# Sink products of two head pairs side by side at half depth, and a new order of the later steps

## The chip, the cores and the metric

The kernel runs on one core of one Trainium2 chip. The metric is the device time of one execution in microseconds (us); less is better. The times shown for a kernel are medians of several executions.

## What is computed

The reference is a windowed attention with sink columns, followed by a gated MLP block that also mixes along the sequence. Sizes: 4 batches, 8 heads, 768 positions, head size 64, so a model width of 512; the MLP is 1024 wide, in two halves of 512. Every query position sees the 4 first positions (the sinks) and the last 128 positions up to itself. All arrays come in as float32.

```python
# attention, for each batch and head
scores = q @ k.T / 8
keep = (pos_k < 4) | ((pos_q - pos_k >= 0) & (pos_q - pos_k < 128))
a = softmax(where(keep, scores, -1e9)); x = a @ v        # heads side by side: x is 768 x 512
# block, for each batch
h = gelu_tanh(x @ w_in); u, v = h[:, :512], h[:, 512:]
v_n = (v - mean(v)) / sqrt(var(v) + 1e-6) * g_ln
v_s = w_sg @ v_n + b_sg[:, None]                         # w_sg is 768 x 768, over positions
out = x + (u * v_s) @ w_out
```

## The kernel before

The work is written as a list of 669 steps, the string `STEPS`. A loop at the end (L675 to L680) runs through it and calls for each step the function of that name, so the list alone sets the order of the instructions on every engine. Each engine takes its own instructions strictly in that order; between engines semaphores make an instruction wait for data and for a buffer to come free. The batches overlap: while TensorE does the block of one batch, the attention of the next is loaded and begun.

The sequence is six tiles of 128 positions, the heads are four pairs (p = 0 to 3). The steps, with b for the batch:

- `LQ.b.i`, `LK.b.i`, `LVH.b.i`, `LWO` are loads. GpSimd (POOL) issues them with a cast to bfloat16, each taking its turn in POOL's queue. `TQ`, `TK` turn q and k with TensorE, `EQ`, `EK` copy the result out of PSUM (suffix A: ScalarE, D: VectorE). In the last batch `DQ`, `DK` turn by DMA, issued by SyncE (SP).
- `QK.b.p.g` (L473) makes the scores of pair p for two query tiles, with the two heads in the two halves of TensorE's rows (64 rows each). `EX` (L486) is the exponential on ScalarE (ACT). `MK` (L490) applies the window mask, on VectorE (DVE, suffix D, L495) or in two instructions on POOL (suffix P, L498 and L501).
- `SK.b.g` (L458) makes the scores of the 4 sink columns of all heads at once for the tiles 2 to 5; head h stands in rows 16h to 16h+3 of one tile, so pair p has rows 32p to 32p+31. `SX` (L465) is their exponential, into `exs`.
- `AV.b.p.k` (L512) multiplies the weights with v into a PSUM tile `mm`: for the batches 1 to 3, k = 0 holds the query tiles 0 to 2 and k = 1 the tiles 3 to 5. For each query tile from 2 on, one product over all 128 rows of `exs` with `v_sink` adds the sinks (L531); `v_sink` is zero outside the pair's own rows. `NR` (L536) divides by the row sums and writes `x_sb` (DVE, two instructions).
- `XD.b.half` (L555) turns `x_sb` by DMA (SP). `MV`, `MU` (L562, L603) are the two halves of x @ w_in, `GV`, `GU` their gelu on ACT; `BN`, `RS`, `NM`, `Z` are the normalization (DVE; `RS` on POOL; `Z` on DVE or ACT by suffix).
- `WT`, `WE` turn w_sg. `SP.b.hf.dc` (L624) is w_sg times the normalized half for three position tiles (hf) and 128 channels (dc); `GT` (L631, DVE) brings it out of PSUM into one of four buffers `gtmp`; `GM` (L636) multiplies with u on DVE or POOL. `OU.b.t` (L640) is the product with w_out, `RA` (L647, DVE) adds x, `ST` and `SH` store (SP). The very last tile is done in two column halves of 256: `OH.3.5.h` (L653), `RH.3.5.h` (L660), `SH.3.5.h`.
- `TBL` (L308) is a one-element activation on ACT, which brings the table of the exponential (E) or of gelu (G) into the engine.

PSUM is two rings: `sc_ring`, two tiles of two banks (`QK`, `MV`, `MU`), and `mm_ring`, four tiles of one bank (everything else). A ring hands out its tiles in the order in which the steps ask (`fresh`, L187). The product that writes into a tile waits for the reader of what that tile held four turns before (two for `sc_ring`). The rings in SBUF work alike, `gtmp` with 4 buffers and `P` (the weights after `EX`) with 10.

Of the kernel before, what the change touches and what calls it, by code (L numbers as in the profile page):

```python
# [40 lines left out]
AV.1.2.1 EX.2.1.0 GM.0.1.2.P NR.1.1.1 AV.1.3.1 NR.1.2.1 QK.2.2.0 LK.3.0 QK.2.3.0 EX.2.2.0 OU.0.1 NR.1.3.1 GM.0.1.3.P  # L41
EX.2.3.0 TBL.G OU.0.2 XD.1.1 RA.0.1 GM.0.1.1.P TK.2.2 MK.2.3.0.D TQ.2.1 LVH.2.0 TQ.2.2 EQ.2.1.D MV.1.0 EQ.2.2.D LQ.3.0
EK.2.2.D LQ.3.1 VSM.2 MU.1.0 GV.1.0 MK.2.1.0.D LVH.2.1 BN.1.0 MV.1.1 GU.1.0 LQ.3.2 RA.0.2 LQ.3.3 MK.2.0.0.D MV.1.2
GV.1.1 MK.2.2.0.D LK.3.1 KS.2 LK.3.2 BN.1.1 MU.1.1 GV.1.2 LK.3.3 BN.1.2 RS.1.1 MU.1.2 GU.1.1 LQ.3.4 NM.1.1 Z.1.0.A
RS.1.2 OU.0.3 GU.1.2 TBL.E LQ.3.5 NM.1.2 Z.1.1.D SK.2.0 Z.1.4.D QK.2.0.1 Z.1.2.D Z.1.3.A QK.2.1.1 Z.1.5.D OU.0.4
# [20 lines left out]
SP.3.0.0 GM.3.1.2.D SP.3.0.1 GT.3.0.0 GT.3.1.3 SP.3.0.2 GT.3.0.1 GM.3.1.3.P SP.3.0.3 GM.3.0.0.D GM.3.0.1.P GT.3.0.2
OU.3.3 GM.3.0.2.D GT.3.0.3 OU.3.4 GM.3.0.3.D RA.3.3 OU.3.0 RA.3.4 ST.3.3 OU.3.1 RA.3.0 ST.3.4 OU.3.2 ST.3.0 RA.3.1
OH.3.5.0 OH.3.5.1 ST.3.1 RA.3.2 ST.3.2 RH.3.5.0 SH.3.5.0 RH.3.5.1 SH.3.5.1
# [8 lines left out]
def kernel(  # L77
# [412 lines left out]
    def MK(b, p, g, e="D"):  # L490
        w = wide(g)
        pt = P[b, p, g]
        if e == "D":
# [4 lines left out]
        nc.gpsimd.affine_select(out=p4[:, :, :, 0:128], in_=p4[:, :, :, 0:128], compare_op=ALU.is_ge,  # L498
                                fill=0.0, base=0, pattern=[[0, 2], [0, 2], [1, 128]],
                                channel_multiplier=-1)  # L500
        nc.gpsimd.affine_select(out=p4[:, :, :, 128:256], in_=p4[:, :, :, 128:256],  # L501
                                compare_op=ALU.is_ge, fill=0.0, base=-1,
                                pattern=[[0, 2], [0, 2], [-1, 128]], channel_multiplier=1)
# [7 lines left out]

    def AV(b, p, k):  # L512
        vb = v_sb[b]
        fresh(mm_ring, ("a", b, p, k))
        av = av_view(b, p, k)
        i0, n = rowsof(b, k)
        first = True
        for il in range(n):
            i = i0 + il
            for hl in range(2):  # L520
# [5 lines left out]
                if i >= 1:  # L526
                    c = 128 if i % 2 else 384
                    nc.tensor.matmul(av[:, il, hl, :], pt[:, hl, c:c + 128], vb[:, h, i - 1, :],  # L528
                                     start=False, stop=(i < 2 and il == n - 1 and hl == 1))
# [186 lines left out]
```

## Time and profile before

| | us |
|---|---|
| median of 3 runs (lowest, highest) | 155.58 (155.23, 155.91) |
| the profiled execution | 155.89 |
| its span, first to last instruction | 154.2 |
| TensorE products (PE) busy | 145.7 |
| VectorE (DVE) busy | 122.9 |
| ScalarE (ACT) busy | 100.0 |
| GpSimd (POOL) busy | 99.7 |

The span starts with the first instruction and ends with the last; 1.7 us of the profiled execution lie around it. Starts are measured. The ends of matmuls are modelled, and a matmul's duration there holds its way through the array, in which the next one already runs. So the pace of a stream of matmuls is read from the starts, and "idle" on PE is less than the gap between two starts.

### The profile page before, as it was taken

The numbers are of one execution on the slowest core, as the hardware profiler recorded it, in microseconds if no ns is written. First come the engines' busy times: TensorE is split into PE (matmuls) and PEld (weight loads), VectorE is DVE, ScalarE is ACT, GpSimd is POOL, SyncE is SP. The second block draws the span as 40 slices with busy tenths as digits, with TensorE's granted clock in tenths as the row PEclk, the third lists the DMA queues.
The fourth block names the chain that finished last, engine by engine and source line by source line (L and its number), as shares of the span: only waits on it lengthen the run. The fifth ranks groups of instructions, "written<-read, shape, count | busy, mean of one in ns | idle before, by whom it ended". The sixth has DMA issues, their size and how long they took to land.

```text
span 154.2 us, 3867 instructions
## 1 busy us (share of the span) xinstructions
PE 145.7 (95%) x1540; PEld 94.5 (61%) x1554; DVE 122.9 (80%) x296; ACT 100.0 (65%) x117; POOL 99.7 (65%) x127
## 2 busy tenths in 40 slices
PE   6899899999999988999899999999999999999990
PEld 2355586879675765758466764486567644775550
DVE  4666889739989977797799887899789957867992
ACT  3699998799899766456987865369957122491000
POOL 4099799298999699999469769640798610400400
PEclk9999999999999999999999999999999999999999
DMA  4999999999999999999999399996510582410055
GB/s 158 305 351 157 154 195 204 166 189 211 148 141 154 185 155 140 147 150 156 156 223 250 81 276 177 185 190 81 211 72 1 105 221 73 150 54 20 0 203 206
DMA packets 87178, 24.67 MB, mean 160 GB/s; under 512 B 78772, under 2 KB 84920, under 8 KB 87160
## 3 DMA queue, kind: packets, MB, share of 16 engines
q0 software_dynamic: 64608, 11.01, 95.7%
q1 hardware_dynamic: 22552, 13.41, 33.0%
q8 instruction: 12, 0.20, 0.5%
q14 instruction: 6, 0.05, 0.1%
HBM read 24.81 MB, written 6.29 MB: 202 GB/s over the span
## 4 chain that ended last, share of the span: by engine, by line
PE 54%; POOL 18%; DMA 15%; ACT 4%; DVE 4%; issue 2%; SPq 1%; DVEq 0%; ACTq 0%; POOLq 0%
PE mm L627 15%; DMA v_sb<-in_v_dram 11%; PE mm L644 10%; PE sc L566 9%; PE sc L607 8%; POOL q L225 5%; POOL k L225 4%; DMA uT<-in_k_dram 4%; PE sc L483 4%; PE mm L524 3%; POOL v_sb L271 3%; PE mm L528 2%; POOL wsg_gated L637 2%; POOL P L498 2%; POOL P L501 2%
## 5 line engine op out<-in xcount | busy, mean ns | idle before, releaser
L488 ACT ACTIVATE P<-sc 128x1024 bf16<-128x1024 f32 (+1 forms) x48 | 43.4, 952 | 10.3 <-PE sc L483 10.1
L627 PE MATMUL mm<-wsgT,z 128*128 128x384 bf16 x192 | 34.4, 327 | 0.3 <-ACT z L597 0.3
L627 PEld LDWEIGHTS <-z 128*128 128x128 bf16 x192 | 17.6, 98 | 12.5 <-issue 0.7
L570 ACT ACTIVATE vt<-sc 128x1024 f32<-128x1024 f32 x12 | 12.3, 1027 | 18.4 <-PE sc L566 18.4
L632 DVE SCALAR_TENSOR_TENSOR gtmp<-mm,g_sb,b_bc 128x384 bf16<-128x384 f32 x32 | 19.0, 610 | 4.2 <-PE mm L627 4.0
L637 POOL TENSOR_TENSOR wsg_gated<-gtmp,uT 128x384 bf16<-128x384 bf16 x15 | 14.9, 1006 | 11.3 <-DVE gtmp L632 11.2
L607 PE MATMUL sc<-xT,w_in_sb 128*128 128x256 bf16 x192 | 22.1, 273 | 0.0
L566 PE MATMUL sc<-w_in_sb,xT 128*128 128x512 bf16 x92 | 21.8, 379 | 0.2
L644 PE MATMUL mm<-w_out_sb,wsg_gated 128*128 128x512 bf16 x85 | 21.2, 379 | 0.5
L498 POOL TENSOR_SCALAR_AFFINE_SELECT P<-P 128x512 bf16<-128x512 bf16 x21 | 13.7, 653 | 11.4 <-ACT P L488 11.4
L607 PEld LDWEIGHTS <-w_in_sb 128*128 128x128 bf16 x192 | 18.7, 98 | 2.9
L579 DVE BATCH_NORM_STATS2 st<-vt 128x6 f32<-128x512 f32 x24 | 15.4, 685 | 6.1 <-ACT vt L570 6.0
L541 DVE TENSOR_TENSOR x_sb<-mm,rcp 128x384 bf16<-128x384 f32 (+1 forms) x36 | 18.5, 513 | 1.2
L588 POOL TENSOR_TENSOR rs<-rs,neg_half 128x4 f32<-128x4 f32 (+1 forms) x8 | 7.1, 882 | 15.8 <-DVE rs L583 14.4
L225 POOL DMA_DIRECT2D k<-in_k_dram x18 | 16.4, 924 | 1.3 <-DMA v_sb<-in_v_dram 1.3
L648 DVE TENSOR_TENSOR ot<-mm,x_sb 128x512 f32<-128x512 f32 x23 | 15.4, 683 | 2.2 <-PE mm L644 2.2
L225 POOL DMA_DIRECT2D q<-in_q_dram x18 | 16.8, 956 | 0.0
L524 PE MATMUL mm<-v_sb,P 128*128 128x65 bf16 x192 | 16.1, 194 | 0.6 <-DVE x_sb L541 0.4
L524 PEld LDWEIGHTS <-P 128*128 128x128 bf16 x192 | 14.5, 97 | 2.5 <-DMA v_sb<-in_v_dram 0.6
L528 PE MATMUL mm<-v_sb,P 128*128 128x65 bf16 x160 | 15.4, 193 | 0.4 <-POOL P L501 0.4
L612 ACT ACTIVATE uT<-sc 128x1024 bf16<-128x1024 f32 x12 | 12.2, 1024 | 5.1 <-PE sc L607 5.1
L566 PEld LDWEIGHTS <-xT 128*128 128x128 bf16 x96 | 9.2, 98 | 10.1
(92 smaller groups left out, 242.9 us busy)
## 6 DMA issues: line engine op xcount, KB each, us to landing
out_dram<-ot SPq DMA_DIRECT2D x17, 256.0 KB, 2.5
v_sb<-in_v_dram POOLq DMA_DIRECT2D x8, 384.0 KB, 8.0
q<-in_q_dram POOLq DMA_DIRECT2D x18, 128.0 KB, 6.5
k<-in_k_dram POOLq DMA_DIRECT2D x18, 128.0 KB, 7.3
out_dram<-ot SPq DMA_DIRECT2D x14, 128.0 KB, 1.8
wsg_gated<-in_moe_w_sg_dram POOLq DMA_DIRECT2D x2, 576.0 KB, 8.4
w_in_sb<-in_moe_w_in_dram POOLq DMA_DIRECT2D x2, 512.0 KB, 9.0
uT<-in_q_dram SPq DMA_DIRECT2D x2, 384.0 KB, 3.0
```

The source lines that it names most:

```text
L225: return nc.gpsimd.dma_start(out=dst.rearrange("p (h d) -> p h d", h=H), in_=heads(src, b, i))
L488: nc.scalar.activation(out=P.new((b, p, g))[:, :, 0:w], in_=sc_ring[b, p, g][:, :, 0:w], func=AF.Exp, scale=scale)
L498: nc.gpsimd.affine_select(out=p4[:, :, :, 0:128], in_=p4[:, :, :, 0:128], compare_op=ALU.is_ge, fill=0.0, base=0, pattern=[[0, 2], [0, 2], ...
L524: nc.tensor.matmul(av[:, il, hl, :], pt[:, hl, c:c + 128], vb[:, h, i, :], start=first, stop=False)
L528: nc.tensor.matmul(av[:, il, hl, :], pt[:, hl, c:c + 128], vb[:, h, i - 1, :], start=False, stop=(i < 2 and il == n - 1 and hl == 1))
L541: nc.vector.tensor_mul(x_sb.get(b)[:, i0:i0 + n, 128 * p:128 * (p + 1)].rearrange("p t (h d) -> p t h d", h=2), av[:, :, :, 0:Dh], rcp[:, ...
L566: nc.tensor.matmul(hp[:, jl, :], xT[b][:, 2 * g + jl, c, :], w_in_sb[:, c, d_half:2 * d_half], start=(c == 0), stop=(c == KD - 1))
L607: nc.tensor.matmul(hp[:, dc // 2, 256 * (dc % 2):256 * (dc % 2 + 1)], w_in_sb[:, c, 128 * dc:128 * (dc + 1)], xT[b][:, 2 * g:2 * g + 2, c, :],
L627: nc.tensor.matmul(ps[:, 0:NH], z[b][:, si, 128 * dc:128 * (dc + 1)], wsgT[:, si, NH * hf:NH * (hf + 1)], start=(si == 0), stop=(si == NT ...
L632: nc.vector.scalar_tensor_tensor(out=gtmp.new((b, hf, dc)), in0=mm_ring["g", b, hf, dc][:, 0:NH], scalar=g_sb[:, dc:dc + 1], in1=b_bc[:, N ...
L637: (nc.vector if e == "D" else nc.gpsimd).tensor_mul(gated(b, hf)[:, dc, :], gtmp[b, hf, dc], uT[b][:, dc, NH * hf:NH * (hf + 1)])
L644: nc.tensor.matmul(ps, gated(b, hf)[:, dc, 128 * tl:128 * (tl + 1)], w_out_sb[:, dc, :], start=(dc == 0), stop=(dc == KU - 1))
```

## The change

Three edits.

**The sink products of batches 1 and 2, tiles 3 to 5.** They leave `AV.b.p.1` and go into a new step `SN.b.p0.1`, ahead of it, which serves the pairs p0 and p0+2: for each of the three query tiles one product over the rows 0 to 63 for the first pair and one over the rows 64 to 127 for the second, into two PSUM tiles. The products of `AV` then add to what is there. A `SN` step asks for both PSUM tiles.

```diff
+    def split(b, k):
+        return k == 1 and b in (1, 2)
+
+    def SN(b, p0, k):
+        i0, n = rowsof(b, k)
+        for p in (p0, p0 + 2):
+            fresh(mm_ring, ("a", b, p, k))
+        for il in range(n):
+            for p in (p0, p0 + 2):
+                rows = slice(64 * (p // 2), 64 * (p // 2) + 64)
+                nc.tensor.matmul(av_view(b, p, k)[:, il, :, :].rearrange("p h d -> p (h d)"),
+                                 exs[b][rows, 128 * (i0 + il - 2):128 * (i0 + il - 1)],
+                                 v_sink[b][rows, 2 * p:2 * p + 2, :].rearrange("p h d -> p (h d)"),
+                                 start=(il == 0), stop=False)
     def AV(b, p, k):
-        fresh(mm_ring, ("a", b, p, k))
+        if not split(b, k):
+            fresh(mm_ring, ("a", b, p, k))
...
-        first = True
+        first = not split(b, k)
...
-            if i >= 2:
+            if i >= 2 and not split(b, k):
```

**The order.** The first 145 steps stay, up to a little behind `XT.0.2`; behind them the computing steps stand in another order. Loads stand in the same order among themselves, and so do the steps of SP. A step's place among the others can move. Some steps change engine: 13 `GM` go from DVE to POOL and 4 back, 3 `MK` from DVE to POOL and 5 back, and some copies and `Z` between ACT and DVE. Four new steps `MK.0.p.g.N` do nothing. `TBL` steps got a number and other places. Two stretches of the new list with the steps spoken of below (lines of the diff, cut):

```diff
...
-MV.0.1 NR.0.3.2 LQ.1.3 BN.0.0 LWS.1 XT.0.2 GV.0.1 MU.0.1 XE.0.2.A BN.0.1 WT.0 GU.0.1 TK.1.0 MV.0.2 RS.0.1 EK.1.0.A
-LK.1.4 NM.0.1 WE.0.A WT.1 GV.0.2 LK.1.5 TK.1.1 MU.0.2 LB.P EK.1.1.A BN.0.2 Z.0.0.A LK.2.0 WT.2 GU.0.2 MU.0.0 WE.1.D
...
-SP.0.1.2 GT.0.1.1 EX.1.1.2 LK.2.4 GM.0.1.0.D AV.1.0.0 MK.1.3.1.D AV.1.1.0 LK.2.5 GM.0.0.3.D QK.1.2.2 GT.0.1.2 QK.1.3.2
-EX.1.2.2 SP.0.1.3 NR.1.0.0 MK.1.1.2.P EX.1.3.2 NR.1.1.0 AV.1.2.0 AV.1.3.0 MK.1.0.2.P GT.0.1.3 QK.2.0.0 QK.2.1.0
-NR.1.2.0 EX.2.0.0 OU.0.0 MK.1.2.2.P NR.1.3.0 TK.2.1 RA.0.0 AV.1.0.1 XD.1.0 EK.2.1.A MK.1.3.2.P AV.1.1.1 NR.1.0.1
...
-OH.3.5.0 OH.3.5.1 ST.3.1 RA.3.2 ST.3.2 RH.3.5.0 SH.3.5.0 RH.3.5.1 SH.3.5.1
+AV.0.2.2 AV.0.3.2 LQ.1.2 NR.0.2.2 GV.0.0 MV.0.1 NR.0.3.2 LQ.1.3 BN.0.0 LWS.1 XT.0.2 GV.0.1 MU.0.1 VSM.1 TK.1.0 LK.1.4
+LK.1.5 XE.0.2.A GU.0.1 BN.0.1 LB.P RS.0.1 MV.0.2 LK.2.0 LQ.2.0 LQ.2.1 WT.0 NM.0.1 GV.0.2 EK.1.0.D Z.0.1.D WT.1 BN.0.2
...
+LQ.2.5 SP.0.1.2 MK.1.1.1.D EX.1.2.1 EX.1.3.1 LK.2.4 MK.1.0.0.D MK.1.0.1.D SP.0.1.1 MK.1.2.0.D MK.1.2.1.P GT.0.1.2
+SX.1.0 QK.1.1.2 QK.1.2.2 EK.2.0.A MK.1.3.1.D EX.1.1.2 SP.0.1.0 AV.1.0.0 TQ.2.0 GT.0.1.1 SP.0.1.3 QK.1.3.2 EX.1.2.2
+GT.0.1.0 GM.0.0.3.P NR.1.0.0 AV.1.1.0 EQ.2.0.D QK.1.0.2 AV.1.2.0 EX.1.3.2 AV.1.3.0 QK.2.1.0 GT.0.1.3 OU.0.0 NR.1.1.0
+EX.1.0.2 NR.1.2.0 TK.2.1 QK.2.3.0 EX.2.1.0 NR.1.3.0 QK.2.0.0 MK.1.0.2.D LK.2.5 SN.1.0.1 MK.1.2.2.P RA.0.0 AV.1.0.1
+MK.1.3.2.P EK.2.1.A AV.1.2.1 XD.1.0 NR.1.0.1 MK.1.1.2.P SN.1.1.1 NR.1.2.1 AV.1.3.1 AV.1.1.1 LK.3.0 EX.2.3.0 QK.2.2.0
+NR.1.1.1 NR.1.3.1 XD.1.1 GM.0.1.1.P GM.0.1.0.P GM.0.1.3.D EX.2.2.0 TQ.2.2 EQ.2.2.A TQ.2.1 LVH.2.0 EX.2.0.0 LQ.3.0
...
+RH.3.5.0 TBL.E.3 OH.3.5.1 SH.3.5.0 RH.3.5.1 SH.3.5.1 TBL.G.4
```

Before, the end of batch 1's normalization stood as `RS.1.1 ... LQ.3.4 ... RS.1.2 ... LQ.3.5` on POOL, now as `RS.1.1 LQ.3.4 LQ.3.5 RS.1.2`. In the last batch the new order on DVE is `BN.3.1 BN.3.2 RA.2.1 NM.3.1` (before: `BN.3.1 BN.3.2 NM.3.1`), on ACT `Z.3.3 Z.3.2 Z.3.1 Z.3.4`, and behind the last `SP` products DVE has `GT.3.0.2 GT.3.0.3 RA.3.3 GM.3.0.3` (before: `GT.3.0.3 GM.3.0.3 RA.3.3`).

**`OH`** takes a new PSUM tile if none is held yet, so that its two halves may come in either order:

```diff
-        ps = mm_ring["o", b, t] if h else fresh(mm_ring, ("o", b, t))
+        ps = mm_ring["o", b, t] if ("o", b, t) in mm_ring.held else fresh(mm_ring, ("o", b, t))
```

More of the change, by code (lines that the diff above doesn't have):

```diff
@@ L41 @@
[L41 to L45, printed above, removed]
@@ L66 @@
[L66 to L68 removed]
+TK.0.0 EQ.0.0.D EK.0.0.A VSO HM.4 QK.0.0.0 ZERO CPK.1.P QK.0.0.1.1 EX.0.0.0 LVH.0.0 EX.0.0.1 MK.0.0.1.N QK.0.0.2.1
+CPQ.1.D TK.0.1 EX.0.0.2 MK.0.0.2.N LC CPQ.2.D LVH.0.1 TQ.0.1 MK.0.0.0.D EK.0.1.A HM.1 TQ.0.2 EQ.0.1.D EQ.0.2.A HM.3
@@ new lines @@
+MV.1.0 MU.1.0 MK.2.3.0.D GV.1.0 MV.1.1 GU.1.0 LK.3.1 BN.1.0 MV.1.2 LK.3.2 GV.1.1 MU.1.1 BN.1.1 LK.3.3 RS.1.1 EK.2.2.A
+GV.1.2 EQ.2.1.A LQ.3.4 BN.1.2 MU.1.2 NM.1.1 OU.0.3 Z.1.3.D GU.1.1 RA.0.3 LQ.3.5 OU.0.4 DK.3.0 RS.1.2 Z.1.0.A DQ.3.0
+NM.1.2 SK.2.0 Z.1.2.D GU.1.2 Z.1.4.D QK.2.0.1 Z.1.1.A QK.2.1.1 TBL.G.2 ST.0.3 EX.2.0.1 Z.1.5.D EX.2.1.1 SX.2.0
+SP.1.1.0 SP.1.1.1 RA.0.4 SP.1.0.1 GT.1.1.1 QK.2.3.1 EX.2.3.1 QK.2.2.1 DQ.3.1 SP.1.1.2 GT.1.1.0 GT.1.0.1 SP.1.0.0
+QK.2.0.2 EX.2.2.1 MK.2.0.1.P QK.2.2.2 MK.2.3.1.D MK.2.1.1.P GM.1.1.1.D GT.1.1.2 MK.2.2.1.P EX.2.0.2 AV.2.0.0
@@ new lines @@
+SP.2.1.2 GM.2.0.1.P GT.2.1.1 ST.1.2 AV.3.3.0 GT.2.1.0 AV.3.1.0 GT.2.1.2 EX.3.0.2 NR.3.3.0 MK.3.1.2.P GM.2.1.1.P
+AV.3.2.0 NR.3.2.0 QK.3.2.2 MK.3.0.2.P EX.3.2.2 QK.3.3.2 NR.3.1.0 SP.2.0.2 EX.3.3.2 GT.2.0.2 SP.2.0.3 AV.3.0.1
+MK.3.2.2.P MK.3.3.2.P GT.2.0.3 AV.3.1.1 GM.2.0.2.P GM.2.1.2.P GM.2.0.3.D GM.2.1.0.P NR.3.0.1 AV.3.2.1 NR.3.1.1
+SP.2.1.3 NR.3.2.1 AV.3.3.1 TBL.E.2 OU.2.2 NR.3.3.1 OU.2.0 GT.2.1.3 XD.3.0 GM.2.1.3.P MV.3.0 OU.2.1 GV.3.0 XD.3.1
+OU.2.5 RA.2.0 RA.2.2 OU.2.3 MV.3.1 GV.3.1 MV.3.2 RA.2.5 BN.3.0 MU.3.0 GV.3.2 RA.2.3 SH.2.0.0 BN.3.1 MU.3.2 BN.3.2
@@ L306, in WARM, with TBL @@
         nc.vector.memset(warm, 0.0)
-    def TBL(func):
+    def TBL(func, turn):
         nc.scalar.activation(out=touch, in_=neg_half[:, 0:1], func=AF.Exp if func == "E" else AF.Gelu_apprx_tanh)
@@ L492, in MK @@
         pt = P[b, p, g]
+        if e == "N":
+            return
         if e == "D":
@@ L528, in AV @@
                     nc.tensor.matmul(av[:, il, hl, :], pt[:, hl, c:c + 128], vb[:, h, i - 1, :],
-                                     start=False, stop=(i < 2 and il == n - 1 and hl == 1))
-            if i >= 2:
+                                     start=False,
+                                     stop=((i < 2 or split(b, k)) and il == n - 1 and hl == 1))
+            if i >= 2 and not split(b, k):
                 nc.tensor.matmul(av[:, il, :, :].rearrange("p h d -> p (h d)"),
```

63 lines of the change are left out of this document (28 added, 35 removed).

## The prediction

> **What bounds the kernel now.** I read the busy shares first, then the busy time by stretch, then the order of time on PE, POOL and DVE, and the chain of waits.
>
> ```profile
> PE 145.7 (95%) x1540; PEld 94.5 (61%) x1554; DVE 122.9 (80%) x296; ACT 100.0 (65%) x117; POOL 99.7 (65%) x127
> ...
> core 0: us, PE busy (x) PEld busy (x) DVE busy (x) ACT busy (x) POOL busy (x), PEclk, DMA share, GB/s
> ...
> 53.50:62.50 9.00, 7.99 (x122) 5.80 (x122) 6.77 (x18) 5.60 (x8) 8.98 (x14) 1.00 1.94 149
> ...
> 75.60:92.00 16.40, 16.03 (x212) 10.32 (x212) 15.19 (x33) 12.51 (x17) 11.45 (x16) 1.00 1.12 206
> ```
>
> TensorE bounds it, at the full granted clock (1.00). In the second of these stretches it rests 0.37 of 16.40 us, in the first 1.01 of 9.00, and there POOL is busy without a break (8.98 of 9.00): TensorE waits for masks and loads that pass through POOL. So the time can fall by the PE work that the change removes and by the few waits, and it rises where the new order makes PE wait anew, or behind the last product.
>
> **The sinks and the change of row mode.** These rows are PE in order of time, one row per run of equal products; then two links of the chain.
>
> ```profile
> 118.76 0.22 PE L531 MATMUL mm<-v_sink,exs 128*128 128x130 bf16 x1
> 118.82 0.19 PE L524 MATMUL mm<-v_sb,P 128*128 128x65 bf16 x1
> ...
> 118.94 0.22 PE L531 MATMUL mm<-v_sink,exs 128*128 128x130 bf16 x1
> ...
> 86.00 0.49 PE L627 MATMUL mm<-wsgT,z 128*128 128x384 bf16 x2
> 86.42 0.50 PE L483 MATMUL sc<-qT,kT 64*128 64x256 bf16 x8
> ...
> 89.67 0.51 PE L483 MATMUL sc<-qT,kT 64*128 64x256 bf16 x8
> 90.10 0.50 PE L627 MATMUL mm<-wsgT,z 128*128 128x384 bf16 x2
> ...
> 20.77 0.45 PE mm L382 x8
> ...
> 100.00 5.24 PE sc L607 x48
> ...
> 137.52 7.80 PE mm L627 x48
> ```
>
> A sink product holds the stream for 0.06 us (118.76 to 118.82), four products with v for 0.12. A product of 256 columns takes 5.24/48 = 0.109, one of 128 columns 0.45/8 = 0.056. The eight products of two `QK` steps at 89.67 are four of each; one after another they would take 0.66 us, two by two 0.33. The next product starts after 0.43. So half-depth products do run two by two, and leaving the 64-row mode costs about 0.10. Entering costs the same: two products of `SP` take 0.33 (7.80/48 = 0.163 each), and at 86.00 the `QK` comes 0.42 after them.
>
> The change takes 24 sink products out (24 x 0.06 = 1.4 us) and puts 12 pairs in at the same 0.06 (0.7): -0.7 us, which is the one bound; the other is 0, if the pairs do not overlap. I take -0.7, because the `QK` row has the same form of product, 64 rows by 128 columns into two banks. Against it stand the changes of mode. I counted the PE steps in both lists from `XT.0.2` to the end, a change wherever neighbours differ in mode (full, 64 rows, and the 32 columns of `SK`): 39 before, 47 after, of these 6 of the 8 new ones ahead of `MV.1.0`. Only some come from `SN`, three of whose four steps stand beside a `QK`; the others come from pairs of `QK` that the order separates. 8 x 0.095 = +0.75. The two cancel within 0.1.
>
> The Trainium skill has a rule against it: "TensorEngine Tiling (Array Packing)", Key Properties, says that changing the tiling mode drains TensorE. It gives no price; "TensorE: Matmul & The Clock Gate", Single matmul latency, puts the part of a product that a stream hides at 166 ns, so by an estimate from that page eight full drains would cost 1.3 us and the sum would be 0.6 higher. The trace agrees that there is a price, and at about 0.10 it is less than a whole drain.
>
> **The waits of before.** PE's own waits, from the list of waits and in order of time:
>
> ```profile
> PE mm L528 <- POOL P L501: 0.4, 1, 0.4
> ...
> 55.07 0.39 PE L382 MATMUL mm<-iden,k 128*128 128x128 bf16 x4
> 55.83 0.40 PE L382 MATMUL mm<-iden,k 128*128 128x128 bf16 x4 [0.37 <-DMA k<-in_k_dram]
> ...
> 75.65 0.76 PE L627 MATMUL mm<-wsgT,z 128*128 128x384 bf16 x3
> 76.67 2.12 PE L627 MATMUL mm<-wsgT,z 128*128 128x384 bf16 x12 [0.26 <-ACT z L597]
> ```
>
> By starts each is some 0.16 longer than the listed idle: 0.53 for k at 55.3 (0.76 less 4 x 0.056), 0.55 for the mask at 58, 0.5 for `Z.1.3.A` at 76.2. Two or three smaller ones (0.2 each, near 54, 73.7 and 88) make it about 2.2 in all, which is the most that order can win.
>
> **Batch 1 in the new order, the place that decides.** POOL in order of time, and the loads of v from the view of v's tile:
>
> ```profile
> 30.67 1.04 POOL L588 TENSOR_TENSOR rs<-rs,neg_half 128x4 f32<-128x4 f32 x1 [3.06 <-DVE rs L583]
> ...
> 49.50 1.03 POOL L637 TENSOR_TENSOR wsg_gated<-gtmp,uT 128x384 bf16<-128x384 bf16 x1
> 51.85 1.82 POOL L225 DMA_DIRECT2D k<-in_k_dram  x2 [1.32 <-DMA v_sb<-in_v_dram]
> 53.67 0.67 POOL L498 TENSOR_SCALAR_AFFINE_SELECT P<-P 128x512 bf16<-128x512 bf16 x1
> ...
> 57.82 0.63 POOL L501 TENSOR_SCALAR_AFFINE_SELECT P<-P 128x512 bf16<-128x512 bf16 x1
> ...
> L271 POOL DMA_DIRECT2D v_sb<-in_v_dram x2: 1452/1456/1459, 40.7 to 42.1; - x2
> ...
> DMA to landing us min/median/max: 7.2/8.2/9.2
> ...
> L632 DVE SCALAR_TENSOR_TENSOR gtmp<-mm,g_sb,b_bc 128x384 bf16<-128x384 f32 x32 | 19.0, 610 | 4.2 <-PE mm L627 4.0
> L541 DVE TENSOR_TENSOR x_sb<-mm,rcp 128x384 bf16<-128x384 f32 x24 | 13.4, 558 | 0.8
> L540 DVE RECIPROCAL rcp<-mm 128x6 f32<-128x6 f32 x24 | 4.5, 186 | 1.2 <-PE mm L531 1.1
> 55.38 0.68 DVE L648 TENSOR_TENSOR ot<-mm,x_sb 128x512 f32<-128x512 f32 x1
> ```
>
> `LK.2.4` waits on POOL until the second load of v has landed (42.1 + 9.2 = 51.3) and starts at 51.85. Behind it before: `LK.2.5` and four masks, 53.67 to 58.45, 1.2 each, and PE waits for the last. After: `MK.1.2.1.P`, `GM.0.0.3.P` (on DVE before), `LK.2.5`, then the other three masks. And `GT.0.1.3` reuses the `gtmp` buffer that `GM.0.0.3` reads, so DVE stands there until POOL is through, with `NR.1.1.0`, `NR.1.2.0`, `NR.1.3.0`, `MK.1.0.2`, `RA.0.0` queued behind; PE waits for these, because `OU.0.0`, `TK.2.1` and both `SN` need the PSUM tiles that they free.
>
> How early `LK.2.4` can start is not in the trace. Three issues (`LK.1.4`, `LK.1.5`, `LB`) now come ahead of `RS.0.1`, in the 3.06 us that POOL waited for it, so v is issued up to 2.4 us earlier. But the two v loads were issued 1.4 apart and landed 3.4 apart: the queue was full. Bounds 0 and 2.4; I take 0.7, nearer to the full queue, so 51.15. Then: `LK.2.4` 0.9 to 52.05, mask 1.2 to 53.25, `GM` 1.0 (49.50) to 54.25. DVE: `GT` 0.61, three `NR` at 0.74, a mask and `RA` at 0.68 each (the row of `RA`; the mask is as long), to 58.5. PE: `SN.1.1.1` with both changes of mode 0.37, two `AV` at 0.36, `QK.2.2.0` with its changes 0.36, three `TQ`/`TK` at 0.45, two `OU` at 0.86 (the row at 145.37 below: 19 in 4.10), in all 4.5: `MV.1.0` starts at 63.0. Before it started at 62.45. So **+0.55 at `MV.1.0`**, with the three waits of the stretch gone and the longer one in their place, the first `SN` pair and the six changes of mode included.
>
> **From there to the last normalization.** The wait for `Z.1.3.A` goes (it stood behind a table load on ACT). But `RS.1.2` now follows `LQ.3.5` and a POOL queue with one more `GM` in it; from the last mask on (54.25, then `LK.2.5` 0.9 and three masks of 1.2: 58.7) it holds ten loads of q and k at 0.91, two of v at 1.46, three `GM` at 1.0, one `RS` of 1.04, and `RS.1.2`:
>
> ```profile
> 35.40 0.72 POOL L588 TENSOR_TENSOR rs<-rs,neg_half 128x2 f32<-128x2 f32 x1 [0.41 <-DVE rs L583]
> ...
> L600 DVE TENSOR_SCALAR z<-vt,rs,nmr 128x512 bf16<-128x512 f32 x15 | 8.0, 586 | 0.0
> ```
>
> That is 75.5, and with DVE's small `NM.1.2` and three `Z` (8.0/15 = 0.53 each) 77.2. PE, some 0.35 later than before, comes to the last tile of z five products after 76.0, at 76.85. So 0.5 becomes 0.3: -0.2. The two small waits: -0.3 (0 to -0.4). The second pair of `SN` steps -0.35, two changes of mode +0.2. Together -0.65; with the +0.55, **-0.1**. In the stretch 75.6 to 92 DVE has 15.19 us of work in 16.40 before; nine `GM` fewer on DVE over the whole give it room, so I put no cost there; without that cover each 0.5 of DVE would count.
>
> In the last batch:
>
> ```profile
> 134.05 0.17 DVE L583 TENSOR_SCALAR rs<-mvs 128x2 f32<-128x2 f32 x1
> ...
> 135.69 1.51 ACT L597 ACTIVATE z<-vt,nmr,rs 128x512 bf16<-128x512 f32 x2
> ```
>
> In before's clock: `BN.3.2` is through at 134.2 (its last instruction, L583), `RA.2.1` (0.68) and `NM.3.1` now follow, so ACT starts at about 135.1, and four `Z` at 0.75 last to 138.1. PE starts `SP.3.1.0` near 137.4 and wants the fifth tile, the last of the four, at 138.0. With the hand-overs I take **+0.25** (0 to 0.9, a whole `RA` and more).
>
> **The end.**
>
> ```profile
> 145.37 4.26 PE L644 MATMUL mm<-w_out_sb,wsg_gated 128*128 128x512 bf16 x19
> 149.47 1.04 PE L657 MATMUL mm<-w_out_sb,wsg_gated 128*128 128x256 bf16 x8
> ...
> L657 PE MATMUL mm<-w_out_sb,wsg_gated x8: 272/272/273, 149.5 to 150.2; 128*128 128x256 bf16 x8
> ...
> 149.67 0.69 DVE L648 TENSOR_TENSOR ot<-mm,x_sb 128x512 f32<-128x512 f32 x1 [0.17 <-PE mm L644]
> 150.55 0.76 DVE L661 TENSOR_TENSOR ot<-mm,x_sb 128x256 f32<-128x256 f32 x2 [0.18 <-PE mm L657]
> 151.00 0.84 SPq L664 DMA_DIRECT2D out_dram<-ot  x2
> ```
>
> Before, `RH.3.5.0` started at 150.55, after all eight products (149.47 + 1.04), though its own half was done at 150.07 (149.47, three paces of 0.109, and 0.27) and DVE was free at 150.36. So the two halves of that PSUM tile are not independent. With the new order `OH.3.5.1` then has to wait for `RH.3.5.0`. The end becomes: `RA.3.2` to 150.36, `RH.3.5.0` 0.42, hand-over 0.06, four products 0.60, hand-over 0.05, `RH.3.5.1` 0.42 = 151.9, against 151.30. **+0.65**, if independent 0. Before it, `RA.3.3` ahead of `GM.3.0.3` makes `OU.3.0` wait about 0.1.
>
> **Sum:** -0.1 + 0.25 + 0.65 + 0.1 = +0.9 on the profiled 155.89, so 156.8. The median of the runs is 0.3 below that execution: 156.5.
>
> **The rivals.** A measurement of this kernel can tell some 0.5%, 0.78 us, from no change.
>
> (1) POOL is early, and the time falls. If v lands the full 2.4 us earlier, `GM.0.0.3` ends at 52.55, DVE never stands, and the three waits before 62.5 (1.3) go with nothing in their place: `MV.1.0` at 62.45 - 1.3 - 0.35 + 0.55 = 61.35, 1.65 earlier than in my sum. Total -0.75: 154.8. It decides at `GM.0.0.3` ending before about 52.7. For it: the 3.06 us in which POOL did nothing. Against it: loads that land 3.4 apart. Chance 0.17, with other ways to be faster.
>
> (2) The halves of the last tile are independent, and the rest is as in my sum: +0.25, 155.8. For it: the code addresses disjoint columns. Against: the start at 150.55. Chance 0.20.
>
> (3) The pairs of `SN` do not overlap, or more of the moved steps wait (13 `GM` are now on POOL at 1.0 us instead of 0.5 on DVE, and DVE waits for their buffers): +0.7 and more beyond my sum, 157.2 to 158. Chance 0.17. Against the first: the `QK` row.
>
> **The numbers.** My forecast has 0.46; of this some 0.33 lie above +0.78. Slower by over 0.5%: 0.33 + 0.17 = 0.50. Within: 0.13 + 0.20 = 0.33. Faster: 0.17. The range 154.7 to 157.9 holds rival (1) and most of (3).
>
> **What would show it.** Right: `SN` products with starts in pairs 0.06 apart; DVE idle before `GT.0.1.3`, released by POOL's `GM`; `MV.1.0` near 63; `OH.3.5.1` starting only after `RH.3.5.0`. Wrong: `MV.1.0` before 62, or the eight products of `OH` back to back.

## The result, and the profile after

| | before | after |
|---|---|---|
| median, us (lowest, highest; 6 runs each) | 155.74 (155.23, 156.93) | 161.78 (160.49, 163.96) |
| profiled execution, us | 155.89 | 162.38 |

The changed kernel is slower, by a ratio of 1.036 with a 95% interval of 1.031 to 1.041. That is 6 us, where the prediction had 0.9 and a range up to 157.9: the sign was right, the size was not.

First the busy shares, then TensorE's busy time and granted clock by stretch (the number ahead of the last two of a row is the clock).

```profile
PE 148.4 (92%) x1540; PEld 95.4 (59%) x1554; DVE 123.5 (77%) x287; ACT 104.1 (65%) x121; POOL 104.2 (65%) x132
...
53.50:66.85 13.35, 10.22 (x138) 7.49 (x137) 10.27 (x22) 6.36 (x8) 13.33 (x17) 0.87 1.52 118
...
60.50:64.00 3.50, 3.50 (x61) 2.94 (x57) 2.88 (x10) 0.81 (x2) 3.50 (x4) 0.62 0.71 62
64.00:68.00 4.00, 3.95 (x29) 2.45 (x29) 3.07 (x7) 1.72 (x2) 4.00 (x5) 0.91 1.92 120
```

The stretch of batch 1 that took 9.00 us before (53.5 to 62.5, where `MV.1.0` started) now takes 13.35, up to `MV.1.0` at 66.85. TensorE rests for 3.1 us of it (1.0 before), and in the 3.5 us after its longest rest it is busy but has a mean clock of 0.62 (before, the whole stretch had 1.00).

Now the same place in order of time, PE, DVE and POOL:

```profile
58.04 0.19 PE L547 MATMUL mm<-v_sb,P 128*128 128x65 bf16 x1
60.17 0.20 PE L543 MATMUL mm<-v_sb,P 128*128 128x65 bf16 x1 [1.94 <-DVE P L498]
...
66.85 1.89 PE L586 MATMUL sc<-w_in_sb,xT 128*128 128x512 bf16 x8
```
```profile
54.93 0.62 DVE L652 SCALAR_TENSOR_TENSOR gtmp<-mm,g_sb,b_bc 128x384 bf16<-128x384 f32 x1 [2.14 <-POOL wsg_gated L657]
...
57.54 2.58 DVE L498 TENSOR_TENSOR P<-P,mask 128x1024 bf16<-128x1024 bf16 x1
60.04 0.68 DVE L668 TENSOR_TENSOR ot<-mm,x_sb 128x512 f32<-128x512 f32 x1
```
```profile
56.97 0.64 POOL L501 TENSOR_SCALAR_AFFINE_SELECT P<-P 128x512 bf16<-128x512 bf16 x1
57.56 0.63 POOL L504 TENSOR_SCALAR_AFFINE_SELECT P<-P 128x512 bf16<-128x512 bf16 x1
58.16 0.63 POOL L501 TENSOR_SCALAR_AFFINE_SELECT P<-P 128x512 bf16<-128x512 bf16 x1
58.75 0.63 POOL L504 TENSOR_SCALAR_AFFINE_SELECT P<-P 128x512 bf16<-128x512 bf16 x1
59.33 0.89 POOL L226 DMA_DIRECT2D k<-in_k_dram  x1
```

The row at 54.93 is the wait that the prediction had: `GT.0.1.3` stands until POOL's `GM` is through. But the mask on DVE behind it, `MK.1.0.2.D`, takes 2.58 us instead of 0.68, and it ends within 0.8 us of the end of POOL's row of masks (59.38). `AV.1.0.1` needs it, so TensorE goes 2.1 us from one start to the next (58.04 to 60.17).

Then two more waits, around `MV.1.1`, and one at the end. PE, ACT, the transpose `XD.1.1` (from the view of its line in the stretch 61 to 65; the three numbers of its first row are the time of the issue in ns), and PE again:

```profile
71.19 1.02 PE L586 MATMUL sc<-w_in_sb,xT 128*128 128x512 bf16 x4 [0.70 <-ACT vt L590]
74.02 2.76 PE L586 MATMUL sc<-w_in_sb,xT 128*128 128x512 bf16 x11 [1.81 <-DMA xT<-x_sb]
```
```profile
68.82 1.28 ACT L590 ACT_TABLE_LOAD   x1 [3.10 <-PE sc L586]
70.12 1.02 ACT L590 ACTIVATE vt<-sc 128x1024 f32<-128x1024 f32 x1
```
```profile
L577 SPq DMA_TRANSPOSE xT<-x_sb x1: 2667/2667/2667, 64.1 to 64.1; - x1
...
DMA to landing us min/median/max: 9.9/9.9/9.9
```
```profile
155.69 0.60 PE L677 MATMUL mm<-w_out_sb,wsg_gated 128*128 128x256 bf16 x4
156.96 0.60 PE L677 MATMUL mm<-w_out_sb,wsg_gated 128*128 128x256 bf16 x4 [0.68 <-DVE ot L681]
```

The gelu table is loaded only when `GV.1.0` comes to run (68.82), since no `TBL.G` stands ahead of it any more: 0.87 us from start to start beyond the pace of the stream. The second half of `MV.1.1` waits 1.97 us for the transpose `XD.1.1`, which lands 9.9 us after its issue; before, it took 5.2. The last row is the tail.

Set side by side by starts, after minus before, PE is +1.40 at `OU.0.0` (0.33 of it from the start-up), +4.40 at `MV.1.0`, +7.24 at `MU.1.2` and +6.20 at `SP.3.1.0`, and the last addition on DVE, `RH.3.5.1`, is +6.70. So nearly all is lost in the some 20 us of batch 1's change-over, 1.0 comes back, 0.5 goes at the tail.

### The profile page after: what moved, and what is told of

Same layout as the page of the kernel before. It is cut to its first block, busy times and chain, and to the rows that moved or that the text cites. A ratio compares the mean times of both kernels' runs of the same rounds, so it can differ in the third digit from the quotient of the medians.

```text
span 160.7 us, 3866 instructions
## 1 busy us (share of the span) xinstructions
PE 148.4 (92%) x1540; PEld 95.4 (59%) x1554; DVE 123.5 (77%) x287; ACT 104.1 (65%) x121; POOL 104.2 (65%) x132
## 4 chain that ended last, share of the span: by engine, by line
PE 65%; DMA 17%; DVE 7%; POOL 4%; issue 3%; SPq 1%; ACT 1%; POOLq 0%; DVEq 0%
PE mm L647 15%; PE sc L586 11%; PE mm L664 11%; PE sc L627 10%; DMA v_sb<-in_v_dram 7%; DMA xT<-x_sb 6%; PE sc L484 5%; PE mm L543 4%; DMA uT<-in_q_dram 4%; PE mm L547 3%; DVE q L201 2%; DVE P L498 2%; PE mm L551 1%; PE mm L383 1%; DVE x_sb L561 1%
## 5 line engine op out<-in xcount | busy, mean ns | idle before, releaser
L657 POOL TENSOR_TENSOR wsg_gated<-gtmp,uT 128x384 bf16<-128x384 bf16 x24 | 22.7, 964 | 10.0 <-DVE gtmp L652 10.0
L498 DVE TENSOR_TENSOR P<-P,mask 128x768 bf16<-128x768 bf16 (+1 forms) x25 | 19.0, 780 | 1.6 <-ACT P L489 1.6
L501 POOL TENSOR_SCALAR_AFFINE_SELECT P<-P 128x512 bf16<-128x512 bf16 x19 | 12.3, 646 | 11.3 <-ACT P L489 7.9
L543 PE MATMUL mm<-v_sb,P 128*128 128x65 bf16 x192 | 15.8, 197 | 1.9 <-DVE P L498 1.9
L543 PEld LDWEIGHTS <-P 128*128 128x128 bf16 x192 | 13.6, 99 | 4.3 <-DVE P L498 2.1
L547 PE MATMUL mm<-v_sb,P 128*128 128x65 bf16 x160 | 15.1, 197 | 0.4 <-POOL P L504 0.4
```

Of the source, the lines that this page charges most:

```text
L657: (nc.vector if e == "D" else nc.gpsimd).tensor_mul(gated(b, hf)[:, dc, :], gtmp[b, hf, dc], uT[b][:, dc, NH * hf:NH * (hf + 1)])
```

## The experiments

All but three are the changed kernel with something undone, moved or added, by its list of steps. A time is the median of the run's executions, and ratios are to the kernel before on the same chip.

**The order at the tail (a_tail).**

```diff
-RH.3.5.0 TBL.E.3 OH.3.5.1 SH.3.5.0 RH.3.5.1
+OH.3.5.1 RH.3.5.0 TBL.E.3 SH.3.5.0 RH.3.5.1
```

> The changed kernel, with only the order of the last four products undone: both OH.3.5 halves first, then RH.3.5.0 and RH.3.5.1. Theory (the two halves share one PSUM tile, so OH.3.5.1 had to wait for RH.3.5.0): the eight products of OH run back to back and the time falls by the 0.65 of the prediction to 0.84 us of idle seen, from 161.8 to about 161.1. Rival (the gap has another cause, the table load or the store): a gap of some 0.8 us stays, 161.8.

161.5 us, ratio 1.038 [1.032, 1.043]. The median can't tell 0.65 us from nothing among runs that spread over 160.8 to 165.3. The trace can: the eight products are one run again.

```profile
157.13 1.04 PE L677 MATMUL mm<-w_out_sb,wsg_gated 128*128 128x256 bf16 x8
```

From the first of these products to the last addition's start are 1.41 us (157.13 to 158.54), as before (149.47 to 150.89, 1.42), against 1.90 in the changed kernel (155.69 to 157.59). So the tail is worth 0.5 us, and its mechanism is as predicted.

**`GM.0.0.3` back on DVE (a_gm).**

```diff
-GT.0.1.0 GM.0.0.3.P NR.1.0.0
+GT.0.1.0 GM.0.0.3.D NR.1.0.0
```

> The changed kernel, with GM.0.0.3 on DVE as before. Theory A (a DVE mask is starved while POOL runs masks back to back): GT.0.1.3 starts near 53.2 instead of 54.93, MK.1.0.2.D starts 1.7 us sooner, near 55.8, but right among POOL's three masks, which then run from about 54.9 to 58.5, so it is stretched again and ends near 58.5 instead of 60.12; AV.1.0.1 starts about 1.5 sooner, PE still rests near 2 us there and its clock still falls: 160 to 160.5. Rival B (the mask was long only because of the late GM on POOL, as in the prediction's chain): it takes 0.7 us, ends at 56.5, PE does not rest, and the time falls by 3 us or more, to 158.5 or below.

159.46 us, ratio 1.016 [1.006, 1.027], its runs spread from 157.1 to 165.5. In the profiled execution, of 157.08, `GT.0.1.3` starts at 53.85 and the mask runs from 56.46 to 58.31: 1.85 us, still stretched, and PE's rest is 1.38. DVE, then the last mask instruction of POOL's row:

```profile
56.46 1.85 DVE L498 TENSOR_TENSOR P<-P,mask 128x1024 bf16<-128x1024 bf16 x1
```
```profile
57.62 1.18 POOL L504 TENSOR_SCALAR_AFFINE_SELECT P<-P 128x512 bf16<-128x512 bf16 x1
```

That is between the two theories in time: the mask is held up as A says, but this time it got through inside the row, ahead of its last instruction, which took 1.18 us for it; only 1.38 us of rest is left, and the clock did not fall behind it. The late `GM`, the whole of the prediction's chain, is thus not the whole of the loss.

**A gap in POOL's masks (a_gap).**

```diff
-MK.1.2.2.P RA.0.0 AV.1.0.1 MK.1.3.2.P ... MK.1.1.2.P ... LK.3.0
+MK.1.2.2.P RA.0.0 AV.1.0.1 LK.3.0 MK.1.3.2.P ... MK.1.1.2.P
```

> The changed kernel, with the load issue LK.3.0 moved ahead of MK.1.3.2.P on POOL; the loads keep their order among themselves. That opens 0.9 us in which POOL touches no SBUF operand. Theory A (starvation): MK.1.0.2.D goes through in that gap, 0.7 instead of 2.58 us, AV.1.0.1 starts near 58.4 instead of 60.16, PE's long rest at 58 shrinks from 2.1 to 0.3 us, and the granted clock behind it stays at 1.00; AV.1.1.1 waits about 0.5 for its mask, now 0.9 later. MV.1.0 from 66.85 to 63.5 to 65, and the time falls by 1.5 to 3 us, to 159 to 160.3 (the late transpose XD.1.1 takes some of it back). Rival B (the mask is long for a reason of its own): still 2.5 us, and the time is 161.8 or higher.

158.21 us, ratio 1.018 [1.012, 1.023]: 3.6 us less than the changed kernel for one load issue moved. DVE, POOL and PE:

```profile
57.35 0.83 DVE L498 TENSOR_TENSOR P<-P,mask 128x1024 bf16<-128x1024 bf16 x1
```
```profile
56.78 0.89 POOL L226 DMA_DIRECT2D k<-in_k_dram  x1
57.67 1.00 POOL L501 TENSOR_SCALAR_AFFINE_SELECT P<-P 128x512 bf16<-128x512 bf16 x1
```
```profile
58.23 0.20 PE L543 MATMUL mm<-v_sb,P 128*128 128x65 bf16 x1 [0.19 <-DVE P L498]
```

The mask starts in the gap and takes 0.83 us, and now POOL's next instruction is the longer one (1.00 instead of 0.64). The clock from 53.5 to `MV.1.0` is 1.00 instead of 0.87. `MV.1.0` starts at 64.17, and the wait for `XD.1.1` is gone as well: it is issued at 62.4 instead of 64.1 and lands after 6.3 us. I had not expected that second part; it made the gain larger than the 1.5 to 3 written down.

**The loads of v out of the way of `XD.1.1` (a_lvh, a_lvh2).** In the first run both stand behind `LQ.3.5`, in the second behind `LK.3.2` and `LK.3.3`.

```diff
-TQ.2.1 LVH.2.0 EX.2.0.0 LQ.3.0 OU.0.2 MK.2.1.0.D LQ.3.1 LVH.2.1 RA.0.2
+TQ.2.1 EX.2.0.0 LQ.3.0 OU.0.2 MK.2.1.0.D LQ.3.1 RA.0.2
...
-LK.3.2 GV.1.1 MU.1.1 BN.1.1 LK.3.3
+LK.3.2 LVH.2.0 GV.1.1 MU.1.1 BN.1.1 LK.3.3 LVH.2.1
```

> The changed kernel, with the two loads of v for batch 2, LVH.2.0 and LVH.2.1, moved from between XD.1.1 and MV.1.0 to behind LQ.3.5. Theory A (the DMA transpose XD.1.1 is slowed by loads that POOL issued shortly before it): it lands 5 to 6 us after its issue instead of 9.9, MV.1.1 has no wait of 1.97 us in its middle, and the time falls by 1.5 to 2, to about 160. Rival B (the transpose is long for another reason, for instance because it is queued behind XD.1.0 or the other loads are as much in its way): it lands near 74 as before and the time stays at 161.8.

166.17 us, ratio 1.068 [1.062, 1.074], a miss by its time: `XD.1.1` landed after 5.2 us and `MV.1.1` did not wait, but `RS.1.2` now stood on POOL behind the two loads, DVE's `NM.1.2` waited for it, and PE for z; behind that rest the clock fell as well (0.50 from 85.40 to 88.80). DVE, then PE:

```profile
82.95 0.16 DVE L611 SCALAR_TENSOR_TENSOR nmr<-mvs,rs 128x2 f32<-128x2 f32 x1 [2.67 <-POOL rs L608]
```
```profile
83.62 0.50 PE L647 MATMUL mm<-wsgT,z 128*128 128x384 bf16 x2 [1.98 <-DVE z L620]
```

So I repeated it with the loads ahead of `RS.1.1`.

> The changed kernel, with LVH.2.0 and LVH.2.1 moved to behind LK.3.2 and LK.3.3, and so ahead of RS.1.1: early enough for v, and not in front of RS.1.2, which held z up by 2.1 us when they stood behind LQ.3.5. Theory A (XD.1.1 is slow beside the loads of v): it lands 5 to 6 us after its issue, MV.1.1 loses its 1.97 us and nothing waits in its place: about 160. Rival B (the transpose keeps its 9.9 us): 161.8.

158.86 us, ratio 1.022 [1.017, 1.028]. The transpose, from the same view as above:

```profile
DMA to landing us min/median/max: 5.4/5.4/5.4
```

It was issued at 63.9, as in the changed kernel, and took 5.4 us without the loads beside it. The rest of 1.97 us is gone; the mask's rest of 2.09 us is still there, and the gain is still 2.9, more than that rest: the clock was full in this execution, by the place of the rest in time (last section), so part of the gain is luck.

**TensorE kept busy while it waits (a_hm).**

```diff
+HM.9 SN.1.0.1 MK.1.2.2.P RA.0.0 AV.1.0.1
```

`HM.9` writes nine products of 512 columns that nobody reads into the next PSUM tile that a step asks for, here that of `SN.1.0.1`, which overwrites them.

> The changed kernel, with nine products of 512 columns that nobody reads (0.216 us each at full clock, 1.94 in all) ahead of SN.1.0.1, where TensorE would stand and wait for the mask MK.1.0.2.D. They add work and remove no wait. Theory A (the rest of 2.1 us on TensorE lowers its clock for the 3.4 us that follow, which costs 1.6): the granted clock from 53.5 to MV.1.0 is 1.00 instead of 0.87, MV.1.0 starts at 65.2 instead of 66.85, and the time falls by 1 to 2 us although TensorE does more. Rival B (the clock fell for another reason, or the products are a pure cost): 161.8 or more.

163.18 us, ratio 1.048 [1.043, 1.052]. Stretches of this run:

```profile
60.50:64.00 3.50, 3.50 (x73) 2.85 (x74) 3.36 (x10) 1.37 (x2) 3.50 (x4) 1.00 0.79 75
...
70.00:74.00 4.00, 2.25 (x8) 0.70 (x8) 1.42 (x4) 0.80 (x1) 2.13 (x3) 0.79 2.89 154
74.00:78.00 4.00, 4.00 (x22) 2.18 (x21) 1.68 (x5) 2.96 (x4) 0.46 (x1) 0.79 2.67 152
```

In its place theory A holds: the clock behind the filled rest is 1.00 instead of 0.62, and `MV.1.0` starts at 65.59 instead of 66.85 (1.7 earlier, reckoned from `XT.0.2`, which was 0.47 later in this run). In the total it does not. In this execution `MV.1.1` still waits 1.91 us for the transpose, and now the clock falls behind that rest, where it had not in the changed kernel: 1.4 us more than there from `MV.1.0` to `MU.1.2`. Another 1.1 goes from there to `SP.3.1.0`, where `MV.2.1` waits for its transpose (103.88). But in two of the four executions the mean clock was 0.998 and 0.999, so that it fell nowhere ahead of the end, and they took 163.22 and 161.83 all the same. A full clock alone did not shorten this kernel, and why those two were no faster stays open.

**The repairs together (c_fix, c_pool).** `c_fix` has the move of `LK.3.0`, `GM.0.0.3.D`, a `TBL.G` behind `EX.2.0.0` and before's tail; `c_pool` has instead of that move the mask on POOL:

```diff
-QK.2.0.0 MK.1.0.2.D LK.2.5 SN.1.0.1
+QK.2.0.0 LK.2.5 MK.1.0.2.P SN.1.0.1
```

> The changed kernel with four repairs: LK.3.0 ahead of MK.1.3.2.P, GM.0.0.3 on DVE, a TBL.G ahead of GV.1.0 (behind EX.2.0.0), and the last four products in before's order. From the run with LK.3.0 alone (157.7 in the profile): less 0.7 for the wait of OU.0.0 for GT.0.1.3, less 0.8 for the tail, less 0.87 for the table load: 155.4, the mask MK.1.0.2.D at 0.7 us and the granted clock at 1.00. Rival (the table load's 0.87 is cover for BN or for the transpose XD.1.1, which would wait in its place): 156.2.

157.09 us, ratio 1.007 [1.003, 1.011], and its ten runs lie between 155.48 and 163.54. The profiled one took 163.43:

```profile
56.58 3.24 DVE L498 TENSOR_TENSOR P<-P,mask 128x1024 bf16<-128x1024 bf16 x1
```

The load issue ran from 55.96 to 56.85, so the mask came 0.27 us before the gap closed, missed it, and waited through two pairs of masks. That in an execution of 155.5 it got through is inferred; none was profiled. PE rested 2.65 us, and 2.85 more at the transpose, each time with half the clock behind it. The `TBL.G` was in its place here: from `MV.1.0` to the first product of `MV.1.1` 3.48 us instead of 4.34, and the wait for the transpose longer by the same 0.9 (2.85 for 1.97). So in the changed kernel the table load cost nothing of its own; the rival was right on that. In `a_lvh2`, where the transpose is on time, its 0.87 us stands alone.

> The changed kernel with four repairs as before, but the mask MK.1.0.2 goes to POOL, behind LK.2.5, in place of the move of LK.3.0 (GM.0.0.3 on DVE, TBL.G ahead of GV.1.0, the last four products in before's order). Theory A (it is the operation on DVE with both operands in SBUF that POOL's masks hold up, and LK.3.0 gave it only an uncertain gap): no run with a long mask any more, no granted clock of 0.98, PE waits some 0.6 for the last of four POOL masks, MV.1.0 near 63.3, 155.8. Rival B (the four masks in a row on POOL delay PE as much): MV.1.0 at 64.5 or later, 157 or more.

155.99 us, ratio 1.003 [1.001, 1.005], all twelve runs between 155.67 and 156.67. As theory A says, with `MV.1.0` at 63.84. Four edits in a list of 677 steps take back 5.6 of the 6.0 us (155.99 beside 155.52 for before on that chip).

**The pairs and the order apart (b_sn, a_nosn, h_ba, h_nosn).** `b_sn` is the kernel before with the `SN` steps ahead of their `AV` steps (`SN.1.0.1` before `AV.1.0.1`, `SN.1.1.1` before `AV.1.1.1`, the pairs of batch 2 behind `QK.3.1.0` and `GT.1.1.3`). `a_nosn` is the changed order without them. `h_ba` has before's steps up to `MV.1.0`, then the changed order with batch 2's pairs and before's tail; `h_nosn` is that without the pairs.

> The kernel before, with the sink pairs alone: SN steps put in front of the AV steps that they serve, all else in before's order. Theory (the pairs overlap, -0.7 for the products; 43 changes of row mode instead of 39, 4 x 0.095 = +0.4): about -0.3, 155.5 beside 155.8. Rival (the pairs do not overlap, or the two PSUM tiles that SN asks for at once make TensorE wait): 156.0 to 156.8.

156.64 us, ratio 1.004 [1.001, 1.008]: the rival. By starts, from `XT.0.2` on, nothing is lost up to `MV.1.0`, and 0.3 in batch 2, where `SN.2.0.1` and `SN.2.1.1` ask for four PSUM tiles in a row and wait for their readers; the other 0.6 by which its profiled run ends later stands already at `XT.0.2`, ahead of any edit.

> The changed kernel's order without the sink pairs: the sink products are back in AV, the SN steps are gone. Theory (the order costs the time, the pairs are worth 0.7 less two of 47 mode changes, 0.2): 0.5 more than the changed kernel where PE is the bound, less where it waits for masks anyway: 161.8 to 162.3. Rival (the pairs themselves cost the time, by their modes or by the two PSUM tiles asked for at once): below 161.

162.1 us, ratio 1.041 [1.034, 1.047]: as the theory has it. The mask took 2.56 us here too (56.87 to 59.43). The pairs did not cost the 6 us.

> The steps of the kernel before up to MV.1.0 (in their order and on their engines), then the remaining steps in the changed kernel's order, with the sink pairs in batch 2 only, and the last four products in before's order. Theory A (all of the loss beyond the tail arises ahead of MV.1.1, and the rest of the new order is worth the 0.65 of the prediction or a little more): MV.1.0 starts at 62.4 as before, the stretch from there to SP.3.1.0 takes 73.9 us (76.71 after, less its two waits of 0.87 and 1.97) against 74.90 before, and the time is about 1.0 below before: 154.7. Rival B (the later order loses too, and its gain is only the catching up of a late TensorE with work that was waiting): 155.7 or more.

154.81 us, ratio 0.995 [0.992, 0.998], 0.5% faster than the kernel before. In this run:

```profile
62.40:74.90 12.50, 12.50 (x87) 7.82 (x84) 10.27 (x26) 9.23 (x10) 12.42 (x13) 1.00 2.17 155
75.60:92.00 16.40, 16.40 (x216) 10.12 (x216) 13.78 (x32) 11.43 (x14) 13.26 (x20) 1.00 1.11 204
...
86.03 0.33 PE L525 MATMUL mm<-v_sink,exs 64*128 64x130 bf16 x6
86.30 0.20 PE L543 MATMUL mm<-v_sb,P 128*128 128x65 bf16 x1
```

TensorE has no rest left in 75.6 to 92 (0.37 before). From `MV.1.0` (62.39) to `SP.3.1.0` (136.37) are 73.98 us, against 74.90: the new order behind `MV.1.0`, with the pairs of batch 2, is worth 0.9, as theory A had it. The last two rows are a pair step: six products and the change of mode behind them in 0.27 us, three paces of 0.06 and one change of 0.10, so the products do run two by two.

> The kernel of before's steps up to MV.1.0 and the changed order behind it, now without the sink pairs of batch 2 too: the new order alone. Theory (a pair step in a place where it does not wait is worth 0.35, less the two changes of mode it brings): 0.1 to 0.3 above the kernel with the pairs (154.8), so 155.0, still below before. Rival (the pairs bring all of that gain): 155.5 or more.

155.24 us, ratio 0.997 [0.994, 1.000]. Beside `h_ba` the pairs of batch 2 are worth 0.4 by the medians, taken on two chips and with intervals that overlap (0.1 to 0.3 was expected); the order alone is not quite told from no change.

## Why the prediction was wrong

**The step that failed** is the list of DVE's work behind `GT.0.1.3`: "three `NR` at 0.74, a mask and `RA` at 0.68 each". The mask took 2.58 us, because POOL ran masks without a break beside it. The rows were copied at their undisturbed length, though the paragraph before put POOL's row of masks beside them, and no bound was given for that. The profile of the kernel before had the sign, in its lines by form:

```profile
L495 DVE TENSOR_TENSOR P<-P,mask 128x1024 bf16<-128x1024 bf16 x8 | 6.3, 793 | 0.0
```

Six of these eight took 0.68 to 0.69 us; two, at 79.98 and 87.13, with POOL computing beside them, took 1.10 and 1.15. "The mask is as long" as `RA` held for the six only. With the mask at 0.83 (`a_gap`) `MV.1.0` came to 64.17 instead of the 63.0 predicted, and of the remaining 1.2 us about 0.5 is an earlier part of the prediction's chain, 0.6 the wait of `AV.1.1.1` for a mask that this run puts later. The earlier part: `LK.2.4` was put at 51.15 and started at 51.88 (51.69 in `a_gap`), so the 0.7 taken for earlier loads was not there, at the lower of its two bounds (the second load of v was issued 1.8 us earlier than before and landed 0.3 earlier, at 51.0), and `GM.0.0.3` ended at 54.89 (54.70) for 54.25. Of the 3.85 us between 63.0 and the 66.85 of the changed kernel, the mask is thus 1.90 and the late `GM` 0.64; the 1.31 left is about what the clock cost.

**What followed from it was not in the sum at all.** The 2.1 us rest lowered the granted clock for 3.4 us, which cost 1.3 to 1.7 (`a_hm` starts `MV.1.0` 1.26 earlier by the starts as they stand, 1.73 from `XT.0.2` on). The late batch brought `XD.1.1` behind `LVH.2.0` (issued at 64.11 and 61.98; before, 59.93 and 62.32), where it took 9.9 us: 1.97 of wait, and the 0.87 of the table load ahead of it. The half clock and the wait for the transpose go when the mask is on time: in `a_gap` and `c_pool` neither is left. The 0.87 stays in `a_gap`, and goes in `c_pool`, which has its `TBL.G` again. `a_hm` shows the clock as a link of its own up to `MV.1.0`, and `a_lvh2` the transpose. Rival (3) had "more of the moved steps wait" with +0.7, the right direction and far too little.

**What held.** The wait of `GT.0.1.3` for POOL's `GM` (2.14 us of idle time on DVE) stands in the trace as predicted. So does `OH.3.5.1` after `RH.3.5.0`: 0.5 by the starts, for 0.65. The stretch from `MV.1.0` on was put at -0.65 with +0.25 for z at `SP.3.1.0`; the runs show -0.9 and no wait for z (73.98 against 74.90), so the +0.25 was not there. The pairs against the changes of mode, "cancel within 0.1": they change the time by between -0.4 (`h_ba` against `h_nosn`) and +0.3 (`b_sn`, where they wait); the overlap and the 0.10 for a change are shown. Rival (1) needed an early POOL, and `LK.2.4` started no earlier than before (51.88 and 51.85). Rival (2) falls with `a_tail`.

## What to carry to other kernels

Before an instruction moves between VectorE and GpSimd, look at what the other engine runs at that moment: an operation on VectorE with both inputs in SBUF has no fixed price beside a row of GpSimd's element-wise work, and one that hangs on a narrow gap can make the time jump from run to run; put it on the same queue, or away from that row. Look for such an operation in the profile that you have: a group whose mean is above its usual length holds some that were held up. When a wait of 2 us on TensorE is forecast, allow for a lower clock behind it, and ask which transfer is issued later because of it and what that then stands behind. An order that loses in one place can still be good elsewhere: split it at a step that both orders share and run the halves.

## What the runs showed of the hardware

**The mask beside POOL.** Over the fourteen profiles of this case, `MK` on DVE at 128x1024 took 0.68 us when POOL computed next to nothing beside it (100 times, at most 0.69). Of the 35 others, 12 had started ahead of a `GM` of POOL and kept 0.68 too, while that `GM` took 1.29; the other 23 took 0.83 to 3.24. `GM` and `KS` on DVE, which also read two tensors in SBUF, are stretched likewise (`GM` 0.35 to 0.62 in the median). Those with an input in PSUM (`NR`, `GT`) and the copies with one input at 128x1024 keep their length. The Trainium skill, "SBUF — State Buffer", section "SBUF: two separate sides", says that such an operation of VectorE and a GpSimd operation that reads SBUF exclude each other for a whole instruction, and that whoever starts first has the ports. The trace agrees on which operations, and the 12 fit who starts first, but the long ones show more than that rule: the mask did not get its turn when the instruction ahead ended, but in 2.58 us let three more of POOL's instructions go first, and in 3.24 us four. In these two it got through when POOL came to something else (a load issue, a `GM`); in `a_gm` it did so inside the row, after two. In `c_fix` it is recorded as started 0.28 us ahead of the first of the four, and still let them pass; in `a_gap` 0.33 us ahead were enough. What decides whose turn it is, no run here shows. A load issue is not always a free gap either: beside load issues alone, masks of 128x768 took 0.83 to 1.26 us instead of 0.55 eleven times.

**The clock.** Eleven rests of TensorE between 1.9 and 2.9 us occur in these profiles behind the start-up, and behind nine of them the granted clock was half for 3.41 us; behind two (1.97 in the changed kernel, 2.09 in `a_lvh2`) it stayed full. The record of the clock shows why. Behind the start-up it changes only at whole steps of 3.41 us, counted from where it first became full: in the changed kernel that was at 6.72, it fell at 61.33, 16 steps later, and rose at 64.75. So the time is best divided at these steps. Here are four such stretches of the changed kernel and two of `a_lvh2`:

```profile
57.92:61.33 3.41, 1.47 (x39) 1.18 (x37) 3.38 (x4) 0.91 (x2) 3.39 (x6) 1.00 0.88 133
61.33:64.74 3.41, 3.41 (x45) 3.01 (x43) 2.82 (x9) 1.55 (x2) 3.41 (x4) 0.50 0.77 53
...
71.57:74.98 3.41, 1.60 (x8) 0.59 (x7) 1.11 (x4) 0.48 (x1) 0.61 (x1) 1.00 2.59 155
74.99:78.40 3.41, 3.36 (x25) 2.28 (x25) 2.03 (x6) 3.25 (x4) 0.39 (x1) 1.00 2.45 155
```
```profile
55.51:58.92 3.41, 2.52 (x30) 1.50 (x29) 3.31 (x8) 2.19 (x3) 3.40 (x6) 1.00 1.84 116
58.93:62.34 3.41, 1.90 (x52) 1.69 (x54) 3.34 (x6) 0.17 (x1) 3.39 (x6) 1.00 1.13 148
```

TensorE is idle for 1.94 us (3.41 less 1.47) of the first stretch, and the next is at half clock. It is idle for 1.81 of the third (the rest that is 1.97 by the starts), and the next is at full clock. In `a_lvh2` the rest falls on the border of two stretches, 0.89 and 1.51 us of idle time, and neither is followed by half clock. In all fourteen profiles, up to the last products, the nine stretches with 1.94 us or more of idle time were each followed by one at half clock, and none with 1.81 or less was. So the same rest costs a half clock or nothing, by where it falls. The Trainium skill, "TensorE: Matmul & The Clock Gate", section "Part 1: The HAM clock gate (the "warmup" mystery)", has half clock after an idle window of some 3.4 us that runs freely. The trace agrees on the length and on the free running; here the window did not have to be idle throughout, 1.94 of its 3.41 us were enough.

**A DMA transpose beside loads.** `XD.1.1` took 3.7 to 5.4 us with no load of v issued in the 4 us before it (seven profiles, `before`, `a_lvh`, `a_lvh2` and `c_pool` among them), 6.3 and 6.6 when it came 0.3 and 0.4 us behind one (`a_gap`, `a_gm`), and 8.1 to 9.9 when it came 1.7 to 3.2 us behind one (five, with 9.9 at 2.1 in the changed kernel). Only the two loads of v were moved on purpose (`a_lvh`, `a_lvh2`), so that it is their bytes and not their place in a queue is not shown.
